# Row decays by small transfers, and a newly laid out order, in a fused linear attention and feed-forward kernel

## The chip, the core and the metric

The kernel runs on one core of a Trainium2 chip, in one launch. The metric is device time in microseconds (us) for one execution; the time before is the median of three. Profiles are of one execution each; their span runs from the first to the last recorded instruction and is a little shorter than the execution's time.

## The reference

Two layers follow each other. The first is a linear attention with a gate for each key element (4 batches, 8 heads, 768 steps, 48 elements a head); the second a gated feed-forward layer (3072 tokens, width 384, hidden width 1536).

```python
f = 1.0 / (1.0 + np.exp(-f_logit))
for t in range(S):
    state = f[:, :, t, :, None] * state + np.einsum('bhd,bhe->bhde', k[:, :, t], v[:, :, t])
    y[:, :, t] = np.einsum('bhd,bhde->bhe', q[:, :, t], state)
x = y.transpose(0, 2, 1, 3).reshape(B * S, H * D)
out = (np.maximum(x @ w_gate, 0.0) * (x @ w_val)) @ w_out
```

All inputs and the output are float32. The kernel multiplies in bf16.

## The kernel before

**Steps, positions, units.** Time is cut into 6 chunks of 128 steps. The work goes in 6 steps c = 0 to 5 of 4 positions b = 0 to 3 each, w = 4c + b. In steps 2 to 5 position b is batch b and the chunk is c. In steps 0 and 1 two positions form a unit: two chunks of one batch, with rows interleaved, so that a load reads 384 bytes a row. Unit 0 is positions 0 and 1 of step 0, unit 1 positions 2 and 3, units 2 and 3 lie in step 1.

**Attention, `front` and `back` (or `unit`).** ScalarE forms log(1 + exp(-f)) (L484, L487). TensorE sums it over the chunk with a triangular matrix (L514; L505 for units) and, with four one-column matmuls (L517; L509 for units), over the whole chunk. ScalarE takes exp(+) for k (L528, `ek`) and exp(-) for q (L530, `eq`), both into the tile `expo`, and from the whole sums the decays of the state (L545; L538 for units) into the tile `dec`. GpSimd (L552) or VectorE (L553) multiplies q and k by them into the tile `hats`. The hats are turned by TensorE (L564) in steps 0 and 1, and by a transposing DMA on SyncE's queue (L572) from step 2 on. Then come the scores (L596; L662 for units), the mask on VectorE (L604, L669), the output y and the state product (L757, L784; L684, L707, L720 for units), and the state update (L454, L458, L460), which reads `dec`.

**Feed-forward.** The four outputs of a step form a group of 512 tokens. For each of 12 hidden blocks there are three gate matmuls and three value matmuls (both L804), a relu on ScalarE (L809) or VectorE (L810) and a product on VectorE (L812). Each output of 128 tokens takes 12 matmuls, in three parts of four (L825), an eviction (L831, L832) and a store (L835). In group 0 the first four hidden blocks are done for each unit by itself, with 256 columns.

**What sets the order.** Each engine runs a list of operations written out by number in `ORDER`. `Plan.link` finds the dependencies from the tiles that an operation reads and writes, `lay_out` places the operations and gives the PSUM banks from `BANKS`, and `waits` makes the semaphore waits. An entry such as `~2512` stands for two matmuls on zeros with 512 columns, which keep TensorE busy. `HELD` adds a dependency by hand: the operation at the left waits for the one at the right. Loads of q, k, v and f go out from SyncE's list or ScalarE's (L408 for units, L413 after), weights from GpSimd's (L435). A list is served in order: what waits at its head holds back all behind it. In the holds before, q of unit 0 (on ScalarE's list) waits for a memset, q of unit 2 for the output of unit 1's second half, v of unit 3 for a transpose of unit 3, and the weight loads `wv2+2`, `wv8+4` and `wo0+4` for operations of group 0.

Weights come in pieces: `wg2+2` is hidden blocks 2 and 3 of the gate, `wg4+4` blocks 4 to 7, and so on.

Of the kernel before, what the change touches and what calls it, by code (L numbers as in the profile page):

```python
# [11 lines left out]
NB, NE, NH, NQ, NM, NV, NA, NN, NS, NX, NG, NR, NO = 3, 3, 6, 6, 5, 6, 3, 4, 2, 2, 2, 4, 3  # L12
UNITS = 4
PE_HATS = set(range(0, 8))
# [11 lines left out]
        45, ~60100, 74, 85, ~3512, 82, ~3512, 90, 80, 92, 121, ~1512, 95, 110, 101, 126, ~4512, 116, ~2512, 100, 128,  # L26
# [14 lines left out]
    ],  # L41
    "ACT": [
# [9 lines left out]
    ],  # L52
    "DVE": [
# [11 lines left out]
    ],  # L65
    "POOL": [
# [4 lines left out]
    ],  # L71
# [9 lines left out]
    48: 10, 57: 114, 60: 140, 67: 284, 69: 164, 70: 185,  # L81
# [161 lines left out]
def bass_hgrn2_outer__then__ffn_reglu_kernel(  # L243
# [11 lines left out]
    C = 128  # L255
# [17 lines left out]
    expo = sb("expo", [128, NE, 2, HD], F32)  # L273
# [14 lines left out]
    decs = sb("dec", [128, NA, B, NP, 2], F32)  # L288
# [6 lines left out]
    tlow = [sb(f"tlow{i}", [128, C], BF16) for i in range(2)]  # L295
    pair = sb("pair", [128, 2], BF16)
    zeros = sb("zeros", [128, 512], BF16)
# [36 lines left out]
    fill("DVE", "zeros", zeros[:], 0.0, 256, -30)  # L334
# [109 lines left out]
    def hq_(i):  # L444
        return f"hq{i}"
# [509 lines left out]
```

## Time and profile before

| | |
|---|---|
| time, median of 3 | 192.87 us (192.62 to 193.22) |
| profiled execution | 193.01 us; span 191.3 us |
| TensorE busy | 180.6 us, 94% of the span |
| VectorE, ScalarE, GpSimd busy | 137.4, 92.0, 59.2 us |
| granted TensorE clock | 1.00 |
| DMA | 32.43 MB moved, 25.95 MB read from HBM |

Engines in the profile: PE is TensorE's matmuls, PEld its weight loads, DVE VectorE, ACT ScalarE, POOL GpSimd, SP SyncE. A row of a group gives the line, the engine, the operation, the tiles and shapes with their count, then busy us and mean ns of one, then the idle time before them and what ended it. A row of the chain or of the timeline gives the start and the length in us. q1 is the queue of SyncE's DMAs, q10 of ScalarE's, q0 of GpSimd's.

### The profile page before, as it was taken

To read this page: it belongs to the slowest core of one execution; us is meant where nothing else is said; L and a number is where in the kernel's file an instruction comes from. 1 tells how busy PE (TensorE), PEld (TensorE's weight loads), DVE (VectorE), ACT (ScalarE), POOL (GpSimd) and SP (SyncE) were. 2 spreads that over 40 slices of the span, in tenths; PEclk is the share of its full clock that TensorE was granted. 3 is DMA by queue.
4 is the path that set the end of the run, shared out by engine and by line. 5 is a ranking of instruction groups with operands and counts; after the bars stand their busy time and mean duration, and the time that the engine had idled before them with its cause. 6 is when DMAs were issued, how large, how long until landed. Compare 5 with 4: busy or idle time off the path is not lost.

```text
span 191.3 us, 4793 instructions
## 1 busy us (share of the span) xinstructions
PE 180.6 (94%) x1977; PEld 108.4 (57%) x1996; DVE 137.4 (72%) x249; ACT 92.0 (48%) x200; POOL 59.2 (31%) x88
## 2 busy tenths in 40 slices
PE   7597999989899999999999999999999999999994
PEld 7364785455655556655555654556656554455562
DVE  4299877986758778669868779988688485655620
ACT  3969663264477546497654574372233132301112
POOL 5638531741036702047371610492600000000000
PEclk9999999999999999999999999999999999999999
DMA  6999999969999999989999999999763300000223
GB/s 163 318 296 216 159 209 264 161 123 251 225 221 206 240 201 246 235 191 200 197 182 215 245 175 175 243 251 178 98 151 108 99 4 0 3 0 0 109 98 126
DMA packets 110278, 32.43 MB, mean 170 GB/s; under 512 B 103472, under 2 KB 110000, under 8 KB 110256
## 3 DMA queue, kind: packets, MB, share of 16 engines
q1 hardware_dynamic: 88960, 25.04, 61.7%
q0 software_dynamic: 3744, 3.54, 12.2%
q10 hardware_dynamic: 17552, 3.54, 10.0%
q8 instruction: 16, 0.26, 0.6%
q14 instruction: 6, 0.05, 0.1%
HBM read 25.95 MB, written 4.72 MB: 160 GB/s over the span
## 4 chain that ended last, share of the span: by engine, by line
PE 85%; DVE 8%; DMA 3%; issue 2%; ACT 0%; DVEq 0%; ACTq 0%
PE ps L804 46%; PE ps L825 25%; DVE hats L553 4%; DMA q_in<-in_q_dram 3%; PE ps L596 2%; PE ps L757 2%; PE ps L564 2%; PE ps L514 1%; DVE gT L812 1%; PE ps L662 1%; PE ps L684 1%; PE ps L784 1%; DVE ptm L669 1%; PE ps L768 1%; PE ps L764 1%
## 5 line engine op out<-in xcount | busy, mean ns | idle before, releaser
L812 DVE TENSOR_TENSOR gT<-relu,ps 128x512 bf16<-128x512 bf16 (+1 forms) x76 | 47.7, 653 | 19.7 <-PE ps L804 17.5
L804 PE MATMUL ps<-xT,wv 128*128 128x512 bf16 (+1 forms) x220 | 53.6, 367 | 0.6 <-issue 0.2
L804 PE MATMUL ps<-xT,wg 128*128 128x512 bf16 (+1 forms) x219 | 52.6, 368 | 0.6
L825 PE MATMUL ps<-wo,gT 128*128 128x384 bf16 (+2 forms) x300 | 52.0, 320 | 0.0
L809 ACT ACTIVATE relu<-ps 128x512 bf16<-128x512 f32 (+1 forms) x42 | 23.9, 576 | 47.8 <-PE ps L804 24.2
L825 PEld LDWEIGHTS ps<-wo,gT 128*128 128x128 bf16 x300 | 27.7, 98 | 18.3
L804 PEld LDWEIGHTS ps<-xT,wg 128*128 128x128 bf16 x228 | 23.6, 108 | 20.5 <-issue 0.4
L804 PEld LDWEIGHTS ps<-xT,wv 128*128 128x128 bf16 x228 | 23.3, 108 | 18.3
L552 POOL TENSOR_TENSOR hats<-q_in,expo 128x384 bf16<-128x384 f32 x17 | 17.9, 1058 | 30.2 <-DMA q_in<-in_q_dram 12.2
L810 DVE TENSOR_SCALAR relu<-ps 128x512 bf16<-128x512 f32 (+1 forms) x34 | 21.7, 654 | 5.4 <-PE ps L804 5.3
L552 POOL TENSOR_TENSOR hats<-k_in,expo 128x384 bf16<-128x384 f32 x17 | 17.7, 1050 | 21.2 <-ACT expo L528 14.9
L604 DVE TENSOR_TENSOR ptm<-ps,tri 128x512 bf16<-128x512 f32 x32 | 20.5, 684 | 5.1 <-PE ps L596 5.1
L831 ACT ACTIVATE osb<-ps 128x384 f32<-128x384 f32 (+1 forms) x16 | 7.6, 484 | 25.0 <-PE ps L825 22.2
L528 ACT ACTIVATE expo<-ps 128x384 f32<-128x384 f32 x24 | 11.7, 496 | 6.1 <-DVE hats L553 2.6
L530 ACT ACTIVATE expo<-ps 128x384 f32<-128x384 f32 x24 | 11.8, 492 | 2.0 <-PE ps L517 1.9
L460 POOL TENSOR_TENSOR st<-ssum,dec 128x384 bf16<-128x384 f32 x10 | 8.6, 864 | 10.0 <-DVE ssum L458 10.0
L669 DVE TENSOR_TENSOR ptm<-ps,tmask 128x512 bf16<-128x512 f32 x16 | 10.0, 678 | 2.1 <-PE ps L662 2.1
L484 ACT ACTIVATE f_in<-f_in 128x768 f32<-128x768 f32 x12 | 10.1, 840 | 2.8 <-DMA f_in<-in_f_logit_dram 2.8
L458 DVE TENSOR_TENSOR ssum<-ps,st 128x384 f32<-128x384 f32 x16 | 8.8, 550 | 2.7 <-PE ps L784 2.5
L553 DVE TENSOR_TENSOR hats<-q_in,expo 128x384 bf16<-128x384 f32 x7 | 8.2, 1167 | 3.4 <-DMA q_in<-in_q_dram 3.4
L487 ACT ACTIVATE bneg<-f_in 128x768 bf16<-128x768 f32 x12 | 10.1, 841 | 1.0 <-ACT osb L831 0.8
L564 PE MATMUL ps<-ident,hats 128*128 128x128 bf16 x64 | 5.5, 220 | 4.0 <-DVE hats L553 3.0
(78 smaller groups left out, 159.2 us busy)
## 6 DMA issues: line engine op xcount, KB each, us to landing
v_in<-in_v_dram SPq DMA_DIRECT2D x12, 384.0 KB, 5.5
out_dram<-osb SPq DMA_DIRECT2D x23, 192.0 KB, 2.3
k_in<-in_k_dram SPq DMA_DIRECT2D x10, 384.0 KB, 7.1
q_in<-in_q_dram SPq DMA_DIRECT2D x9, 384.0 KB, 5.8
f_in<-in_f_logit_dram SPq DMA_DIRECT2D x8, 384.0 KB, 4.8
f_in<-in_f_logit_dram ACTq DMA_DIRECT2D x4, 384.0 KB, 6.6
q_in<-in_q_dram ACTq DMA_DIRECT2D x3, 384.0 KB, 5.6
wv<-in_moe_w_val_dram POOLq DMA_DIRECT2D x2, 384.0 KB, 6.7
```

The costliest lines, as they stand in the source:

```text
L484: add(f"ef{c}{b0}", by("ACT", lambda: sc.activation(raw, raw, AF.Exp, scale=-1.0), act_(n)), keys, keys, key=P)
L528: add(f"ek{c}{b}", by("ACT", lambda: sc.activation(ex[:, 1, :], bc.ap[:, 0:HD], AF.Exp, scale=1.0), act_(HD)), [bc], [f"expk{ei}"], key=P + 1)
L530: add(f"eq{c}{b}", by("ACT", lambda: sc.activation(ex[:, 0, :], bc.ap[:, 0:HD], AF.Exp, scale=-1.0), act_(HD)), [bc], [f"expq{ei}"], key=P ...
L552: return {**by("POOL", lambda: gp.tensor_tensor(o, i_, e_, ALU.mult), pool_(HD)), **by("DVE", lambda: ve.tensor_tensor(o, i_, e_, ALU.mult ...
L553: **by("DVE", lambda: ve.tensor_tensor(o, i_, e_, ALU.mult), dve_(HD))}
L604: add(f"m{c}{b}{j}", by("DVE", lambda b=b, j=j, mi=mi: ve.tensor_tensor(ptm[mi][:, j, :, :], s[b, j].ap[:, :].rearrange("p (n t) -> p n t" ...
L669: add(f"m{c}{b2[i]}{j}", by("DVE", lambda i=i, j=j, mask=mask: ve.tensor_tensor(ptm[mi[i]][:, j, :, :], s[j, i].ap[:, :].rearrange("p (n t ...
L804: z = te.matmul(bank.ap[:, 0:n], wt[:, kt, w_cols(j)], xT[xi][:, kt, n0:n1], start=(kt == 0), stop=(kt == NK - 1))
L809: add(f"r{c}{b0}.{j}", {**by("ACT", lambda: sc.activation(rdst, gate.ap[:, 0:n], AF.Relu), act_(n)), **by("DVE", lambda: ve.tensor_scalar_ ...
L810: **by("DVE", lambda: ve.tensor_scalar_max(rdst, gate.ap[:, 0:n], 0.0), dve_(n))}, [gate], [f"relu{ri}"], key=P)
L812: add(f"p{c}{b0}.{j}", by("DVE", lambda: ve.tensor_tensor(gT[gi][:, j, n0:n1], rdst, val.ap[:, 0:n], ALU.mult), dve_(n)), [val, f"relu{ri} ...
L825: z = te.matmul(o.ap[:, 0:e1 - e0], gT[gi][:, j, b * C:(b + 1) * C], wo[:, j, e0:e1], start=(j == 0), stop=(j == NJ - 1))
```

## The change

**Row decays.** For positions w = 8 to 19 (steps 2 to 4) the four one-column matmuls and the ScalarE exponentials into `dec` are left out. The exp(-) of a pair of positions is written into one interleaved tile, element (d, j, position, p), so that one row holds what the decays need: the last row of the chunk is the whole sum. A new operation `xd`, two DMAs a pair of positions, copies that row from partition 127 to 48 partitions each, eight floats to a partition:

```diff
+ROW_DECAYS = set(range(8, 20))
+NEQ = 2
-            if c < NC - 1:
+            if ch < NC - 1 and not rows:
                 for p in range(NP):
                     x = te.matmul(bc.ap[:, HD + p:HD + p + 1], ... ones[:, :])
...
-        ex = expo[:, ei, :, :]
+        ex = (expq[:, eqi, :, :].rearrange("q x h -> q (x h)").rearrange("q (d j x p) -> q x p j d", d=D, x=2, j=2)[:, b % 2, :, :, :] if rows
+              else expq[:, eqi, b % 2, :].rearrange("q (p j d) -> q p j d", p=NP, j=2),
+              expk[:, ei, :].rearrange("q (p j d) -> q p j d", p=NP, j=2))
...
+        elif rows and b % 2:
+            b0, c0 = place(c, b - 1)
+            def decay_rows(eng):
+                for j in range(2):
+                    at, to = expq[C - 1:C, eqi, 0, 2 * NP * j:2 * NP * j + 1], decs[64 * j:64 * j + D, ai, j, b0, 0:1]
+                    x = eng.dma_start(bass.AP(tensor=to.tensor, offset=to.offset, ap=[list(to.ap[0]), [1, 2 * NP]]),
+                                      bass.AP(tensor=at.tensor, offset=at.offset, ap=[list(at.ap[0]), [4 * NP, D], [1, 2 * NP]]))
+            xd = add(f"xd{c}{b - 1}", {**by("SP", ...), **by("ACT", ...)}, [f"expq{eqi}_0", f"expq{eqi}_1", f"dec{ai}"], [f"dec{ai}_{b0}", f"dec{ai}_{bt}"], key=P + 2)
```

**Tiles.** `expo` (three buffers for both kinds) becomes `expk` with two buffers and `expq` with two pairs. `dec` is stored with the head's half ahead of batch and head pair. `zeros` is 128 columns wide and is read repeatedly for wider fills; `tlow` lies in one buffer of `ssum`. `place` and `load` are written so that more units would be possible; with four the addresses are the same.

**Orders, banks, holds.** `ORDER` and `BANKS` are new in full. The parts that the prediction speaks of:

- SyncE's list begins with f of units 0 and 1, then k, v and q of unit 0, q of unit 1, f of units 3 and 2, k and v of unit 1, k of units 2 and 3, q and v of unit 3, q and v of unit 2, then all f, k, q and v of step 2 on its list and f of step 3: 24 loads ahead of the first store. Before, it began with f of units 0 and 1, k and v of unit 0, k, v and q of unit 1, and q of unit 0 was on ScalarE's list.
- `HELD` keeps `wv8+4` (now behind another relu of group 0) and gains k of steps 4 and 5 in one pair each; the holds of q of units 0 and 2, v of unit 3, `wv2+2` and `wo0+4` are gone.
- ScalarE's list begins exp f, log (unit 0), exp f (unit 1), `ek` of position 1, log (unit 1), decays of unit 0, `ek` and `eq` of position 0. Before, `eq` and `ek` of position 0 came right after exp f of unit 1.
- GpSimd's list after the memsets: hat of q 0, `wg2+2`, hat of q 3, `wv2+2`, hats of q 2, k 2, k 3, a state update, `wg0+2`, v, `wv0+2`, v, hats of k 10 and 11, `wg4+4`. Before: `wg2+2`, hat of k 1, k 3, v, `wv2+2`, hat of q 2, `wg0+2`, `wv0+2`, `wv4+4`, `wg4+4`, `wg8+4` (numbers are step and position).
- TensorE's fills are 12, 2, 2, 2 and 9 matmuls of 512 columns, where before there were 60 of 100 and 3, 3, 1, 4 and 2 of 512. The nine stand between the state product of unit 0 and the transposes of unit 1. The transposes of units 2 and 3 stand among and before the projections of group 0's first four blocks; before they stood behind most of group 0's projections.
- Group 0's relus: 12 on ScalarE and 4 on VectorE, before 8 and 8.
- The six `xd` stand on SyncE's list (20/21, 22/23, 32/33) and on ScalarE's (30/31, 40/41, 42/43). The first stands between the first store and the transposes of step 2.

More of the change, by code (lines that the diff above doesn't have):

```diff
@@ L272, in bass_hgrn2_outer__then__ffn_reglu_kernel @@
     bneg = sb("bneg", [128, NB, 2, H, 64], BF16)
-    expo = sb("expo", [128, NE, 2, HD], F32)
+    expk, expq = sb("expk", [128, NE, HD], F32), sb("expq", [128, NEQ, 2, HD], F32)
     hats = sb("hats", [128, NH, 2, H, 64], BF16)
@@ L287, in bass_hgrn2_outer__then__ffn_reglu_kernel @@
     osb = [sb(f"osb{i}", [128, DM], F32) for i in range(NO)]
-    decs = sb("dec", [128, NA, B, NP, 2], F32)
+    decs = sb("dec", [128, NA, 2, B, NP], F32)
     dec = [decs[:, i, :, :, :] for i in range(NA)]
@@ L294, in bass_hgrn2_outer__then__ffn_reglu_kernel @@
     tmask = [sb(f"tmask{i}", [128, C], BF16) for i in range(2)]
-    tlow = [sb(f"tlow{i}", [128, C], BF16) for i in range(2)]
+    tlow = [ssum[NS - 1][:, C // 2 * i:C // 2 * (i + 1)].bitcast(BF16) for i in range(2)]
     pair = sb("pair", [128, 2], BF16)
-    zeros = sb("zeros", [128, 512], BF16)
+    zeros = sb("zeros", [128, 128], BF16)
     banks = [nc.alloc_psum_tensor(f"ps{i}", [128, 512], F32) for i in range(8)]
@@ L332, in select @@
         add("s" + name, by("POOL", lambda: gp.affine_select(out=ap, in_=ap, **kw), (0.24, 0.29)), [name], [name], key=key)
-    fill("DVE", "zeros", zeros[:], 0.0, 256, -30)
+    fill("DVE", "zeros", zeros[:], 0.0, 64, -30)
     fill("POOL", "tri", tri[:], 1.0, 128, -12 if UNITS else -20)
@@ L450, in new_state @@
         t4 = lambda t: t[:, 0:HD].rearrange("p (n j e) -> p n j e", n=NP, j=2)
-        rate = dec[ai][:, b, :, :].unsqueeze(3).to_broadcast([128, NP, 2, D])
+        rate = dec[ai][:, :, b, :].rearrange("q j p -> q p j").unsqueeze(3).to_broadcast([128, NP, 2, D])
         dk = [f"dec{ai}_{b}", f"dec{ai}"]
@@ L470, in front @@
         w = c * B + b
-        two, cc, bt = w < 2 * UNITS, w // 2 // B * 2, w // 2 % B
+        two, (bt, ch) = w < 2 * UNITS, place(c, b)
+        cc = ch - b % 2
         P = w * 10
         bi, bj = (w // 2) % NB, w % 2
-        ei, hi, qi, ai = w % NE, w % NH, w % NQ, c % NA
+        ei, eqi, hi, qi, ai = w % NE, w // 2 % NEQ, w % NH, w % NQ, ch % NA
         fin, kin, qin, vins = (halves(n, slot_of(n, c, b // 2)) if two else ld[n][:, slot_of(n, c, b // 2), :, :, 0:D] for n in "fkqv")
@@ L495, in front @@
         bn = bneg[:, bi, bj, :, :]
+        rows = w in ROW_DECAYS
         onto = two and bj and w // 2 in ONTO
@@ L523, in front @@
         else:
-            add(f"cum{c}{b}", pe(cum, mm(HD) + (mm(1) * 4 if c < NC - 1 else 0)), ["tri", "ones", f"bneg{bi}", f"bn{bi}_{bj}"], [bc],
+            add(f"cum{c}{b}", pe(cum, mm(HD) + (mm(1) * 4 if ch < NC - 1 and not rows else 0)), ["tri", "ones", f"bneg{bi}", f"bn{bi}_{bj}"], [bc],
                 key=P, opens=[bc])
-        ex = expo[:, ei, :, :]
-        add(f"ek{c}{b}", by("ACT", lambda: sc.activation(ex[:, 1, :], bc.ap[:, 0:HD], AF.Exp, scale=1.0), act_(HD)), [bc],
+        ex = (expq[:, eqi, :, :].rearrange("q x h -> q (x h)").rearrange("q (d j x p) -> q x p j d", d=D, x=2, j=2)[:, b % 2, :, :, :] if rows
+              else expq[:, eqi, b % 2, :].rearrange("q (p j d) -> q p j d", p=NP, j=2),
+              expk[:, ei, :].rearrange("q (p j d) -> q p j d", p=NP, j=2))
+        parts = lambda t: t.rearrange("q (p j d) -> q p j d", p=NP, j=2)
+        past = []
+        if w >= 2 * NEQ and rows != (w - 2 * NEQ in ROW_DECAYS):
+            w0 = w // 2 * 2 - 2 * NEQ
+            names = {f"hq{x // B}{x % B}" for x in (w0, w0 + 1)} | {f"xd{w0 // B}{w0 % B}"}
+            past = [o for o in pl.ops if o.name in names]
+        add(f"ek{c}{b}", by("ACT", lambda: sc.activation(ex[1], parts(bc.ap[:, 0:HD]), AF.Exp, scale=1.0), act_(HD)), [bc],
             [f"expk{ei}"], key=P + 1)
-        add(f"eq{c}{b}", by("ACT", lambda: sc.activation(ex[:, 0, :], bc.ap[:, 0:HD], AF.Exp, scale=-1.0), act_(HD)), [bc],
-            [f"expq{ei}"], key=P + 1)
+        add(f"eq{c}{b}", by("ACT", lambda: sc.activation(ex[0], parts(bc.ap[:, 0:HD]), AF.Exp, scale=-1.0), act_(HD)), [bc],
+            [f"expq{eqi}_{b % 2}"], key=P + 1, after=past)
         if two and bj == 0:
@@ L541, in front @@
             add(f"dc{c}{b}", by("ACT", decay2, (0.24, 0.35)), [bc, f"dec{a0}", f"dec{a0 + 1}"], [f"dec{a0}_{bt}", f"dec{a0 + 1}_{bt}"], key=P + 2)
-        elif c < NC - 1 and not two:
+        elif rows and b % 2:
+            b0, c0 = place(c, b - 1)
+            assert c0 == ch and bt == b0 + 1
+            def decay_rows(eng):
[3 more added lines that the diff above has]
+                                      bass.AP(tensor=at.tensor, offset=at.offset, ap=[list(at.ap[0]), [4 * NP, D], [1, 2 * NP]]))
+                    if j == 0:
+                        x.then_inc(xd.sem, 16)
+                return x
+            xd = add(f"xd{c}{b - 1}", {**by("SP", lambda: decay_rows(sy), (0.8, 0.8)), **by("ACT", lambda: decay_rows(sc), (0.8, 0.8))},
+                     [f"expq{eqi}_0", f"expq{eqi}_1", f"dec{ai}"], [f"dec{ai}_{b0}", f"dec{ai}_{bt}"], key=P + 2)
+            dma(xd, f"dec{ai}_{b0}", "SP", 6, 0.013)
+            slots[f"dec{ai}_{b0}"][1] += 16
+            xd.goal += 16
+        elif rows:
+            pass
+        elif ch < NC - 1 and not two:
             def decay():
                 for j in range(2):
-                    x = sc.activation(dec[ai][64 * j:64 * j + 64, b, :, j], bc.ap[64 * j:64 * j + 64, HD:HD + NP], AF.Exp, scale=-1.0)
+                    x = sc.activation(dec[ai][64 * j:64 * j + 64, j, bt, :], bc.ap[64 * j:64 * j + 64, HD:HD + NP], AF.Exp, scale=-1.0)
                 return x
-            add(f"dc{c}{b}", by("ACT", decay, (0.23, 0.34)), [bc, f"dec{ai}"], [f"dec{ai}_{b}"], key=P + 2)
+            add(f"dc{c}{b}", by("ACT", decay, (0.23, 0.34)), [bc, f"dec{ai}"], [f"dec{ai}_{bt}"], key=P + 2)
         def scaled(src, xh, xe):
-            o, e_ = hats[:, hi, xh, :, 0:D], ex[:, xe, :].rearrange("p (h d) -> p h d", h=H)
-            i_ = src[:, b % 2, :, :]
+            o, e_ = hats[:, hi, xh, :, 0:D].rearrange("q (p j) d -> q p j d", p=NP), ex[xe]
+            i_ = src[:, b % 2, :, :].rearrange("q (p j) d -> q p j d", p=NP)
             return {**by("POOL", lambda: gp.tensor_tensor(o, i_, e_, ALU.mult), pool_(HD)),
@@ L554, in front @@
         add(f"hk{c}{b}", scaled(kin, 1, 1), in_k("k") + [f"expk{ei}", f"hats{hi}"], [hk_(hi)], key=P + 2)
-        add(f"hq{c}{b}", scaled(qin, 0, 0), in_k("q") + [f"expq{ei}", f"hats{hi}"], [hq_(hi)], key=P + 2)
+        add(f"hq{c}{b}", scaled(qin, 0, 0), in_k("q") + [f"expq{eqi}_{b % 2}", f"hats{hi}"], [hq_(hi)], key=P + 2)
         if w in PE_HATS:
@@ L736, in back @@
         P = w * 10
+        bt, ch = place(c, b)
         hi, qi, mi, vi, xi = w % NH, w % NQ, w % NM, w % NV, c % NX
@@ L768, in natural @@
                 z = te.matmul(y.ap[:, h * D:(h + 1) * D], ptm[mi][:, h % 2, h // 2, :], vp[:, at:at + D],
-                              start=(c == 0 and h == 0), stop=True, skip_group_check=True)
+                              start=(ch == 0 and h == 0), stop=True, skip_group_check=True)
             return z
@@ L887, in run @@
                     eng.wait_ge(sems[d.eng], d.val)
+                n = fill % 1000
+                row = zeros[:, 0:n] if n <= 128 else zeros[:].unsqueeze(1).to_broadcast([128, n // 128, 128])
                 for _ in range(fill // 1000):
-                    te.matmul((op.opens[0].ap if op.opens else banks[7])[:, 0:fill % 1000], zeros[:, 0:128], zeros[:, 0:fill % 1000],
+                    te.matmul((op.opens[0].ap if op.opens else banks[7])[:, 0:n], zeros[:], row,
                               start=True, stop=True, skip_group_check=True)
```

38 lines of the change are left out of this document (22 added, 16 removed), and 102 rows, old and new, of tables (BANKS, ORDER).

## The prediction

> **What bounds the kernel now.** I read the page's shares first, then the busy time by stretches, TensorE's waits, the chain of the first 10 us, and last the DMA queues.
>
> ```profile
> span 191.3 us, 4793 instructions
> PE 180.6 (94%) x1977; PEld 108.4 (57%) x1996; DVE 137.4 (72%) x249; ACT 92.0 (48%) x200; POOL 59.2 (31%) x88
> PE 85%; DVE 8%; DMA 3%; issue 2%; ACT 0%; DVEq 0%; ACTq 0%
> ```
>
> The profiled execution took 193.01 us, 1.7 more than its span and 0.14 more than the median of 192.87; sums below are against 193.0. TensorE sets the time. Its idle time lies where the stretches show it (columns: length, then busy us of PE, PEld, DVE, ACT, POOL, then granted clock, DMA share, GB/s):
>
> ```profile
> 5.00:10.00 5.00, 2.72 (x35) 1.64 (x33) 1.79 (x3) 4.47 (x9) 2.81 (x7) 1.00 1.17 312
> 15.00:20.00 5.00, 3.54 (x140) 2.54 (x141) 4.97 (x9) 4.67 (x9) 4.76 (x6) 1.00 0.99 182
> 30.00:40.00 10.00, 9.78 (x55) 5.10 (x54) 9.96 (x13) 4.03 (x9) 5.71 (x7) 1.00 1.02 196
> 40.00:50.00 10.00, 9.22 (x120) 5.69 (x120) 7.58 (x16) 4.51 (x9) 2.01 (x4) 1.00 0.93 197
> 50.00:60.00 10.00, 9.40 (x228) 5.80 (x229) 6.78 (x13) 6.83 (x14) 3.30 (x4) 1.00 1.36 231
> 60.00:70.00 10.00, 9.95 (x55) 5.33 (x55) 7.43 (x13) 5.54 (x15) 5.38 (x6) 1.00 0.98 199
> ```
>
> Three regions lose time: the front of the first two units (to 20 us), 30 to 60 us (1.6 us idle: 0.22, 0.78, 0.60), and the drain. From 60 us on almost nothing is idle. So a change can gain only by taking matmuls away, or by ending waits before 60 us:
>
> ```profile
> PE ps L564 <- DVE hats L553: 3.0, 2, 1.9
> PE ps L564 <- DVE gT L812: 0.8, 1, 0.8
> PE ps L684 <- issue: 0.5, 1, 0.5
> ```
>
> L564 are the transposes of the scaled q and k: TensorE waits for VectorE's multiplications. VectorE is the crowded engine there (9.96 of 10 us in 30 to 40).
>
> **Part 1: row decays, steps 2 to 4.** The change takes out L517, four one-column matmuls behind each of 12 cumulative sums, and L545, the ScalarE exponentials that read them.
>
> ```profile
> 53.28 0.34 PE L514 MATMUL ps<-bneg,tri 128*128 128x384 bf16 x1
> 53.45 0.24 PE L517 MATMUL ps<-ones,bneg 128*128 128x1 bf16 x4
> 53.55 0.81 PE L825 MATMUL ps<-wo,gT 128*128 128x384 bf16 x4
> L517 PE MATMUL ps<-ones,bneg 128*128 128x1 bf16 x48 | 2.9, 164 | 0.0
> L545 ACT ACTIVATE dec<-ps 64x4 f32<-64x4 f32 x24 | 4.0, 166 | 1.1 <-PE ps L517 0.9
> ```
>
> Matmuls overlap, so 2.9 us busy is the upper bound. The four start at 53.45 and the next operation at 53.55: 0.10 us a sum, 12 x 0.10 = 1.2 us of TensorE, nearly all of it after 53 us where TensorE is full. I take -1.2 (bounds -2.9 and 0). ScalarE loses 4.0 us of work, worth nothing by itself at 48% busy.
>
> It adds six transfers of two DMAs each (three pairs on SyncE's queue, three on ScalarE's). They read one row of the exponentials; what waits for them is the state update, a whole set of masks and scores later. Behind the first of them on SyncE's queue stand the transposes of step 2, whose hats are ready later than those exponentials anyway. The trace has no DMA that small. The nearest is the smallest store, which lands in 1.6 us; the transposes, which lie behind them on SyncE's queue, take 3.3:
>
> ```profile
> out_dram<-osb SPq DMA_DIRECT2D x1, 64.0 KB, 1.6
> qkT<-hats SPq DMA_TRANSPOSE x16, 3.3
> L552 POOL TENSOR_TENSOR hats<-q_in,expo 128x384 bf16<-128x384 f32 x17 | 17.9, 1058 | 30.2 <-DMA q_in<-in_q_dram 12.2 <-ACT f_in L484 11.3 <-ACT expo L530 6.7
> 175.59 1.30 PE ps L825 x8
> 149.72 9.66 PE ps L804 x44
> ```
>
> The tightest place I find in the new order is the pair 42/43: between its cumulative sums and its scores lie 16 projections of three L804 matmuls and 4 output parts of four L825 matmuls, 48 x 0.22 + 16 x 0.16 = 13.1 us. The chain in it is four exponentials (2 us), two decay issues, GpSimd's hats (1.06 each, one behind a value load), the transposes (two issues, 3.3 to land): 9 to 10 us. Cover of 3 us, so zero; if it is gone, its overrun is paid in full. The two buffers of k's exponentials instead of three make an exponential wait for the hat two positions before it, which stands ahead of it by several GpSimd operations: zero by the same cover.
>
> The row layout makes q's exponentials a stride of 64 bytes for ScalarE's write and for the multiplication. No row shows that stride; bounds are 0 and a doubling of 1.06 us, and I take the middle, +0.5 a hat, hidden by those 3 us. [...]
>
> **Part 2: unit 0's loads in one queue, and ScalarE's new order.**
>
> ```profile
> 2.54 5.55 DMA q_in<-in_q_dram
> 8.19 1.29 DVE hats L553
> 9.52 0.40 PE ps L564 x4
> 7.10 0.87 ACT L528 ACTIVATE expo<-ps 128x384 f32<-128x384 f32 x2
> 5.10 0.84 ACT L487 ACTIVATE bneg<-f_in 128x768 bf16<-128x768 f32 x1
> 14.80 0.36 ACT L538 ACTIVATE dec<-ps 64x8 f32<-64x8 f32 x2
> q1 hardware_dynamic: 1357, 0.52, 101.7%
> q1 hardware_dynamic: 861, 0.32, 117.1%
> 11.86 0.64 PE L662 MATMUL ps<-qkT 48*64 48x128 bf16 x32
> 19.84 0.50 PE L804 MATMUL ps<-xT,wg 128*128 128x256 bf16 x3
> ```
>
> Today q of unit 0 lands last (8.1) and starts the chain. As fifth load in SyncE's queue it is complete after 5 x 0.39 MB. The queue moved 0.52 MB by 4 us (first q1 row, 2 to 4 us) and 0.32 MB a us when full (second, 8 to 9 us): 4 + 1.45 / 0.32 = 8.5. But ScalarE, free of its first exponential at 7.1, now runs the second logarithm and the decays before the exponentials of position 0: 7.1 + 0.8 + 0.3 + 0.9 = 9.1, so the later load is covered. GpSimd then multiplies until 10.1, and with the transposes and copies the first scores (L662) come at 11.7 to 12.3, against 11.86. The second half's k comes ninth instead of fifth (about 14.5), and GpSimd's hats behind it push the first projection (L804) to about 20.3, against 19.84. The nine idle fills of 512 columns ahead of those transposes (9 x 0.22 = 2.0 us from about 13.2) end before the hats, so cost nothing unless the state product ahead of them is late. By then the new order has also done three cumulative sums, 1.2 us of work. Net -0.7; chains added by hand leave small waits out, so I take -0.3, bounds -1.0 and +0.8.
>
> **Part 3: 28 to 55 us, and the weights.** VectorE is relieved: of group 0's 16 relus it keeps 4 instead of 8 (ScalarE takes 12), and of the first four units' 16 hats 5 instead of 8. The transposes of units 2 and 3 stand some 10 us of TensorE work earlier. So the L564 waits there (1.1 for hats, 0.8 for gT) should shrink: of the 1.6 us idle I take 0.9 away (bounds 0 and 1.6). Against that stands the loss of two holds. SyncE now keeps back q of unit 2, with all that is queued behind it, to 23.98 us, and v of unit 3 to 42.3; the new order issues 24 loads without a wait, beside the weights.
>
> ```profile
> 23.98 0.37 SPq L408 DMA_DIRECT2D q_in<-in_q_dram  x1
> 42.30 0.99 SPq L408 DMA_DIRECT2D v_in<-in_v_dram  x2
> q0 software_dynamic: 580, 0.57, 120.1%
> ...
> q1 hardware_dynamic: 1393, 0.53, 99.6%
> 28.83 0.81 PE L804 MATMUL ps<-xT,wg 128*128 128x512 bf16 x3
> q0 software_dynamic: 3744, 3.54, 12.2%
> wg<-in_moe_w_gate_dram POOLq DMA_DIRECT2D x2, 384.0 KB, 9.0
> ```
>
> The third and fourth rows are queues in 24 to 27 and in 28 to 30 us (packets, MB, share of the engines): a load issued at 23.98 got nothing while the weights (q0) were queued, and all engines after. Requests are served in blocks, roughly as issued, so a weight waits for the two or three loads ahead of it and then has the engines. With GpSimd's work before it the first 384 KB weight goes out at about 21.9 (19.4 today) and lands, by the same 9.0 or, without the other weights ahead of it, some 2 less, at 28.9 to 30.9; its first use is due at about 28.6 (28.83 today). GpSimd's hat of q, position 11, waits for the fifteenth load, about 31, which may cost TensorE 0.6. Together +0.8 (0 to +3). Part 3 is -0.9 + 0.8 = -0.1.
>
> Sum: -1.2 - 0.3 - 0.1 = -1.6; 193.0 - 1.6 = 191.4. The drain keeps its last three steps, zero.
>
> **Rivals.** (a) *Weights late, slower.* If the unheld loads get their share first, the last gate and value columns land 3 to 6 us after their use is due (about 36 to 41 us), TensorE waits there, and nothing returns it: 191.4 and 3 to 6 gives 194.4 to 197.4, 195 the nearest. It decides once each weight lands over 8 us after its issue. For: 24 loads of 0.39 MB and the weights (3.54 MB written, twice that read as float32) need about 50 us at 0.32 MB a us. Against: the blocks above. [...] Chance 0.20. (b) *The saving is eaten*: new waits of 1 to 2 us in the re-laid order, as the old one has 1.6; 192.3 to 193.8, chance 0.14. (c) *The stride slows the hats* until the scores of pair 42/43 wait: 3 us of cover gone and 2.4 more, 193.8; for it only the doubled hat, four of them in a row; against it GpSimd's 31% share. Chance 0.04. (d) *All early waits end*: a further 1.5, 189.9; chance 0.12.
>
> **How the numbers follow.** The forecast, 190.4 to 192.3, has 0.50. About 0.3% (0.6 us) can be told from no change. Faster: 0.50 + 0.12 = 0.62. Of (b) 0.10 lies within 0.3%, 0.04 above; slower is 0.20 + 0.04 + 0.04 = 0.28. The range 189.9 to 195.2 leaves out part of (d) and the worse part of (a), under 2 in 10.
>
> **What would show it.** Right: L517 gone and TensorE's busy time 1 us less after 53 us; first projection near 20.3; 30 to 60 us with under 1.5 us idle. Wrong: L804 of group 0 waiting for wg or wv between 28 and 45 us; transposes waiting for the small DMAs on SyncE's queue; L596 (scores) idle in step 4; hats above 1.5 us.

## The result, and the profile after

The changed kernel takes 190.8 us (median of 4, 190.59 to 191.51) against 192.93 before (192.62 to 193.22), a ratio of 0.989 [0.9852, 0.9927]. On another chip, with more runs of the kernel before beside it, it took 191.27 (six runs) and the ratio was 0.9885 [0.9847, 0.9923]. The forecast was 191.4 in 189.9 to 195.2. (The first run of `e8_relu_dve` took 314.01 us at a granted clock of 0.56; the ratios in this document leave it out, and with it a few executions that were slower at a slightly lower clock, which the medians include.)

The page after, its span and shares, for an execution of 190.59 us:

```profile
span 188.9 us, 4607 instructions
PE 182.4 (97%) x1902; PEld 104.9 (56%) x1902; DVE 133.9 (71%) x246; ACT 91.9 (49%) x179; POOL 60.7 (32%) x88
```

TensorE's busy time is higher than before, though 48 matmuls are gone. That is no riddle: fills take 9.0 us where they took 7.5, and the trace of before holds 439 of the 456 gate and value projections, that of after all. So busy totals of the two aren't compared; idle stretches and experiments are. (A record that is missing leaves a gap of only 0.05 us, as at 35.85 us of the kernel before, where two of three projections are recorded.) The same view by stretches as in the prediction, from 20 us on:

```profile
20.00:25.00 5.00, 3.66 (x99) 2.51 (x99) 4.06 (x8) 3.30 (x8) 5.00 (x8) 1.00 1.30 267
30.00:40.00 10.00, 10.00 (x114) 5.67 (x113) 8.78 (x17) 4.07 (x9) 3.09 (x5) 1.00 1.22 211
40.00:50.00 10.00, 10.00 (x225) 6.01 (x224) 6.62 (x13) 6.84 (x12) 0.00 (x0) 1.00 0.97 191
50.00:60.00 10.00, 10.00 (x52) 5.01 (x51) 5.75 (x9) 5.65 (x11) 8.03 (x9) 1.00 1.12 218
```

The 1.6 us of idle TensorE between 30 and 60 us are gone (0.1 of them were missing records), and from there to 180 us nothing is idle. One hole is new, 20 to 25 us. TensorE's waits name it:

```profile
PE ps L842 <- DMA wg<-in_moe_w_gate_dram: 1.1, 1, 1.1
PE ps L601 <- POOL hats L589: 0.2, 1, 0.2
```

L842 is the line of the projections (L804 before), L601 that of the transposes (L564). The transposes' 3.8 us of waiting for VectorE has become 0.2 for GpSimd, and a wait for a gate weight is new. But 3.0 of the 3.8 stood in the front, at 9.52 us (1.85) and, in the kernel before, here:

```profile
17.64 0.61 PE L564 MATMUL ps<-ident,hats 128*128 128x128 bf16 x8 [1.17 <-DVE hats L553]
```

Only the 0.8 for `gT`, at 40.78 us, lie between 30 and 60 us. In the front other work and fills stand where those 3.0 us were. The changed kernel, in order of time:

```profile
11.76 0.64 PE L699 MATMUL ps<-qkT 48*64 48x128 bf16 x32 [0.60 <-DVE qkT L605]
19.93 0.83 PE L842 MATMUL ps<-xT,wg 128*128 128x256 bf16 x6
23.30 0.83 PE L842 MATMUL ps<-xT,wg 128*128 128x256 bf16 x6 [1.13 <-DMA wg<-in_moe_w_gate_dram]
```

The first scores come at 11.76 and the first projection at 19.93 us, as before to 0.1 us, with three more cumulative sums done. The wait at 23.30 is for `wg0+2`, issued at 16.77 and landed at 23.3, 6.5 us later.

### The profile page after: what moved, and what is told of

Same layout as the page of the kernel before. It is cut to its first block, busy times and chain, and to the rows that moved or that the text cites. A ratio compares the mean times of both kernels' runs of the same rounds, so it can differ in the third digit from the quotient of the medians.

```text
span 188.9 us, 4607 instructions
## 1 busy us (share of the span) xinstructions
PE 182.4 (97%) x1902; PEld 104.9 (56%) x1902; DVE 133.9 (71%) x246; ACT 91.9 (49%) x179; POOL 60.7 (32%) x88
## 4 chain that ended last, share of the span: by engine, by line
PE 86%; DMA 6%; SPq 3%; POOL 2%; ACT 1%; issue 0%
PE ps L842 49%; PE ps L863 25%; DMA wg<-in_moe_w_gate_dram 3%; SPq L411 3%; DMA f_in<-in_f_logit_dram 3%; PE ps L633 2%; PE ps L795 2%; POOL hats L589 2%; PE ps L524 1%; PE ps L822 1%; PE ps L721 1%; PE ps L601 1%; PE ps L806 1%; PE ps L802 1%; PE ps L699 1%; PE ps L757 0%
## 5 line engine op out<-in xcount | busy, mean ns | idle before, releaser
L842 PE MATMUL ps<-xT,wv 128*128 128x512 bf16 (+1 forms) x228 | 56.1, 368 | 0.0
L842 PE MATMUL ps<-xT,wg 128*128 128x512 bf16 (+1 forms) x228 | 54.7, 368 | 1.2 <-DMA wg<-in_moe_w_gate_dram 1.1
L847 ACT ACTIVATE relu<-ps 128x512 bf16<-128x512 f32 (+1 forms) x47 | 26.7, 577 | 49.0 <-PE ps L842 46.7
L842 PEld LDWEIGHTS ps<-xT,wg 128*128 128x128 bf16 x228 | 23.7, 108 | 21.3 <-DMA wg<-in_moe_w_gate_dram 1.5
L842 PEld LDWEIGHTS ps<-xT,wv 128*128 128x128 bf16 x228 | 23.5, 108 | 18.9
L848 DVE TENSOR_SCALAR relu<-ps 128x512 bf16<-128x512 f32 (+1 forms) x29 | 18.9, 658 | 9.7 <-PE ps L842 9.6
L589 POOL TENSOR_TENSOR hats<-k_in,expk 128x384 bf16<-128x384 f32 x17 | 16.9, 999 | 26.2 <-ACT expk L546 26.1
L589 POOL TENSOR_TENSOR hats<-q_in,expq 128x384 bf16<-128x384 f32 x15 | 17.8, 1190 | 19.0 <-ACT expq L548 12.5
L641 DVE TENSOR_TENSOR ptm<-ps,tri 128x512 bf16<-128x512 f32 x32 | 20.3, 683 | 2.3 <-PE ps L633 2.1
L869 ACT ACTIVATE osb<-ps 128x384 f32<-128x384 f32 (+2 forms) x18 | 8.6, 480 | 22.1 <-PE ps L863 20.7
L548 ACT ACTIVATE expq<-ps 128x384 f32<-128x384 f32 x24 | 15.5, 669 | 0.0
L546 ACT ACTIVATE expk<-ps 128x384 f32<-128x384 f32 x24 | 11.8, 498 | 2.0 <-PE ps L524 1.3
L646 ACT ACTIVATE xT<-ps 128x384 bf16<-128x384 f32 x10 | 5.1, 535 | 9.6 <-PE ps L795 5.9
L619 POOL CAST vpad<-v_in 128x384 bf16<-128x384 f32 x12 | 6.9, 588 | 8.9 <-DMA v_in<-in_v_dram 8.9
## 6 DMA issues: line engine op xcount, KB each, us to landing
out_dram<-osb SPq DMA_DIRECT2D x23, 192.0 KB, 2.2
```

What stands on the lines that cost most here:

```text
L546: add(f"ek{c}{b}", by("ACT", lambda: sc.activation(ex[1], parts(bc.ap[:, 0:HD]), AF.Exp, scale=1.0), act_(HD)), [bc], [f"expk{ei}"], key=P ...
L548: add(f"eq{c}{b}", by("ACT", lambda: sc.activation(ex[0], parts(bc.ap[:, 0:HD]), AF.Exp, scale=-1.0), act_(HD)), [bc], [f"expq{eqi}_{b % 2 ...
L589: return {**by("POOL", lambda: gp.tensor_tensor(o, i_, e_, ALU.mult), pool_(HD)), **by("DVE", lambda: ve.tensor_tensor(o, i_, e_, ALU.mult ...
L641: add(f"m{c}{b}{j}", by("DVE", lambda b=b, j=j, mi=mi: ve.tensor_tensor(ptm[mi][:, j, :, :], s[b, j].ap[:, :].rearrange("p (n t) -> p n t" ...
L842: z = te.matmul(bank.ap[:, 0:n], wt[:, kt, w_cols(j)], xT[xi][:, kt, n0:n1], start=(kt == 0), stop=(kt == NK - 1))
L847: add(f"r{c}{b0}.{j}", {**by("ACT", lambda: sc.activation(rdst, gate.ap[:, 0:n], AF.Relu), act_(n)), **by("DVE", lambda: ve.tensor_scalar_ ...
```

## The experiments

| kernel | median us | before, same chip | ratio of the two |
|---|---|---|---|
| e1_keep_sums | 192.38 | 193.16 | 0.9975 [0.9944, 1.0005] |
| e2_no_rows | 192.22 | 193.16 | 0.9964 [0.9937, 0.999] |
| e3_rows_old | 204.12 | 193.16 | 1.0566 [1.0503, 1.0628] |
| e6_wg_first | 191.08 | 193.16 | 0.9911 [0.9879, 0.9943] |
| e3b_rows_old_act | 197.86 | 193.42 | 1.0192 [1.0143, 1.0242] |
| e5_old_no_holds | 196.50 | 193.42 | 1.0136 [1.0092, 1.0179] |
| e8_relu_dve | 193.88 | 193.42 | 1.0024 [1.0001, 1.0046] |
| e9_weights_first | 190.58 | 193.42 | 0.9851 [0.9814, 0.9887] |
| a0_changed | 191.27 | 193.78 | 0.9885 [0.9847, 0.9923] |
| e10_hold_step2 | 190.77 | 193.78 | 0.9857 [0.9823, 0.9892] |
| e8b_relu_dve | 193.15 | 193.78 | 0.9987 [0.995, 1.0023] |
| e7_q0_act | 191.75 | 193.78 | 0.9908 [0.9873, 0.9944] |

**The matmuls, put back into the changed kernel.**

```diff
-            if ch < NC - 1 and not rows:
+            if ch < NC - 1:
```

> The changed kernel (190.8 us), with the 48 one-column matmuls of steps 2 to 4 put back; their results are not read. Theory (TensorE is never idle from 30 us on, so its work sets the time): 12 x 0.10 us more, 192.0. Rival (the one-column matmuls were hidden and the gain comes from the new order alone): 190.8.

It took 192.38, by the ratios 0.85% or 1.6 us more than the changed kernel, so the one-column matmuls cost what the theory said and a little over. The start times in its timeline confirm the 0.10 us a sum (L524 is the sum, L527 the four matmuls):

```profile
49.99 0.24 PE L527 MATMUL ps<-ones,bneg 128*128 128x1 bf16 x4
50.09 0.32 PE L524 MATMUL ps<-bneg,tri 128*128 128x384 bf16 x1
...
59.12 0.84 PE L842 MATMUL ps<-xT,wv 128*128 128x512 bf16 x3 [0.83 <-DVE relu L848]
```

The last row is what the matmuls cost beside their own time: a projection at 59 us now waits 0.8 us for a relu.

**The new order without row decays.**

```diff
-ROW_DECAYS = set(range(8, 20))
+ROW_DECAYS = set()
```

with the 24 exponentials into `dec` back in ScalarE's list, behind those of k and q, and no `xd`.

> The new order without row decays: sums by matmuls, decays by ScalarE right behind the exponentials of their position, no small transfers, no interleaved layout. Theory: only the matmuls count, 192.0, as in e1. Rival 1 (ScalarE's 4 us of decays matter too): 192.5 or more. Rival 2 (the interleaved layout slows ScalarE and the hats and costs time): 191.5 or less.

192.22, near the theory's 192.0 and between the two rivals. It is 1.4 us more than the changed kernel, and 0.7 less than before (0.2 to 1.2 by its interval). Here the split is clean: no new wait of any size, and TensorE's row has the difference (182.4 in the changed kernel):

```profile
PE 184.0 (97%) x1950; PEld 106.3 (56%) x1950; DVE 133.7 (70%) x246; ACT 92.3 (48%) x203; POOL 58.1 (31%) x88
```

So, taken away from the changed kernel, the row decays are two thirds of the gain, and the order without them is one third. Between the two kernels only the row layout and the decays differ, which prices the layout too. First the groups of this kernel, then those of the changed one:

```profile
L548 ACT ACTIVATE expq<-ps 128x384 f32<-128x384 f32 x24 | 11.6, 497 | 0.1
L589 POOL TENSOR_TENSOR hats<-q_in,expq 128x384 bf16<-128x384 f32 x15 | 15.5, 1038 | 17.9 <-ACT expq L548 12.6 <-DMA q_in<-in_q_dram 5.2
```

```profile
L548 ACT ACTIVATE expq<-ps 128x384 f32<-128x384 f32 x24 | 15.5, 669 | 0.0
L589 POOL TENSOR_TENSOR hats<-q_in,expq 128x384 bf16<-128x384 f32 x15 | 17.8, 1190 | 19.0 <-ACT expq L548 12.5 <-DMA q_in<-in_q_dram 6.3
```

The strided write costs ScalarE 3.9 us over 12 exponentials (0.8 us each instead of 0.5), and the 4.0 us of decay exponentials that it saves are gone with it: ScalarE's total is 91.9 against 92.3. Of the seven strided hats of q on GpSimd four take 1.19 us, two 1.5 and one 1.8, instead of 1.0.

**The row decays in the old order, with the transfers on SyncE's list.** Order, banks and holds of before; k's exponentials have three buffers, q's two pairs as in the changed kernel; each transfer stands just ahead of the first transpose of its pair (lists by names):

```diff
 # SyncE
+xd20 ahead of the first of xh20, xh21; xd22, xd30, xd32, xd40, xd42 likewise
 # ScalarE
-dc20 dc21 ... dc43
```

> The old order with row decays alone (three buffers of k's exponentials; each small transfer on SyncE's list ahead of the first transpose of its pair). Theory: 192.9 - 1.2 = 191.7. Rival (in an order not made for them the transfers or the slower layout delay the transposes of steps 2 to 4, and scores wait): 192.9 or more.

204.12, 11 us slower than before. The theory fell. The rival's time came, but not by late transposes or scores: ScalarE's waits and one row of its timeline tell why:

```profile
ACT expq L539 <- DMA dec<-expq: 10.1, 2, 6.6
...
94.84 0.81 ACT L539 ACTIVATE expq<-ps 128x384 f32<-128x384 f32 x1 [6.58 <-DMA dec<-expq]
...
PE ps L833 <- ACT osb L860: 4.5, 1, 4.5
PE ps L833 <- ACT expq L539: 2.5, 1, 2.5
```

A pair's tile comes free only when its transfer has landed, and that transfer stood behind loads and stores in SyncE's list. So an exponential waits 6.6 us, and behind it in ScalarE's list wait an eviction and relus, for which TensorE waits. That is 7.0 us of waiting. After the longer wait the granted clock fell as well:

```profile
95.00:102.00 7.00, 5.97 (x18) 2.45 (x19) 0.56 (x1) 3.15 (x7) 0.00 (x0) 0.51 0.98 218
```

Seven us at 0.51 are about 3.4 us of full clock lost. So, by this estimate, about a third of the 9.5 us by which this execution is longer (202.53 against 193.01) comes through the clock.

**The same, with the transfers on ScalarE's list**, right behind the exponentials that they read. The buffers are those of the run above (the three buffers that the expectation gives to q's exponentials are k's).

```diff
 # SyncE
-xd20 xd22 xd30 xd32 xd40 xd42
 # ScalarE
+each behind the second exponential of q of its pair
```

> The order, banks and holds of the kernel before, with the row decays of steps 2 to 4; all six small transfers stand on ScalarE's list, right behind the exponentials that they read, and q's exponentials have three buffers. Theory (what made the earlier attempt slow was the place of the transfers on SyncE's list, behind loads and transposes, and not the transfers or the layout): nothing is queued ahead of a transfer, so it lands 3 to 5 us after its exponentials, TensorE loses 1.2 us of one-column matmuls, and the time is 191.3 to 192.2 us, with ScalarE's exponentials waiting for a transfer by under 1 us. Rival 1 (the layout or the transfers themselves cost time in an order not made for them): 192.9 or more, up to the 204 of the earlier attempt, with TensorE waiting for q's exponentials or for GpSimd's hats of q. Rival 2 (the old order's idle time swallows the saving): 192.9 within 0.5, TensorE 1 us less busy and 1 us more idle.

197.86: the theory fell. Rival 1's time came, but by another wait than it names (TensorE for q's exponentials or hats): the transfers land soon (2.7 us median), but their issue occupies ScalarE. First ScalarE here, then the same place in the kernel before:

```profile
57.75 2.24 ACTq L557 DMA_DIRECT2D dec<-expq  x2
60.03 0.84 ACT L486 ACTIVATE bneg<-f_in 128x768 bf16<-128x768 f32 x1 [2.32 <-issue]
...
61.02 0.32 PE L514 MATMUL ps<-bneg,tri 128*128 128x384 bf16 x1 [1.99 <-ACT bneg L486]
```

```profile
57.30 0.84 ACT L487 ACTIVATE bneg<-f_in 128x768 bf16<-128x768 f32 x1
```

The two small DMAs hold the list for 2.24 us, the logarithm comes 2.7 us later than before, and the cumulative sum waits 2 us for it. That is one of several such places; TensorE is also idle by 1.1 us in 90 to 100 us and 0.9 in 100 to 110, and not each of these is traced. What is shown: the row decays are worth 1.4 us in the order laid out for them, and cost 4 to 11 us in one that isn't.

**The old order without its holds on loads.** Rival (a), priced where it can be.

```diff
-    48: 10, 57: 114, 60: 140, 67: 284, 69: 164, 70: 185,
+    48: 10, 57: 114, 69: 164, 70: 185,
```

(60 is q of unit 2, 67 v of unit 3.)

> The kernel before, without its holds of q of unit 2 and v of unit 3, so that SyncE issues these loads and all behind them without a wait, beside the weights. Theory (a weight in GpSimd's queue is served before the loads that are queued beside it, so the loads suffer and the weights do not): 192.5 to 194, TensorE's waits for wg or wv together under 1 us, and loads of q and f that take 10 us and more to land. Rival (the queues share, so unheld loads delay the weights; rival a of the prediction): 195 to 198, with L804 waiting 2 us or more for wg or wv between 18 and 45 us.

196.5, by the ratio 2.6 us slower than before: the rival holds. TensorE waits for weights, and the last three of the four gate loads (issued 17.0 to 20.1 us) take longer to land. The first block is this run, the second the kernel before:

```profile
PE ps L804 <- DMA wg<-in_moe_w_gate_dram: 1.7, 1, 1.7
PE ps L804 <- DMA wv<-in_moe_w_val_dram: 0.9, 1, 0.9
...
DMA to landing us min/median/max: 8.0/12.6/14.5
```

```profile
DMA to landing us min/median/max: 5.4/8.2/9.9
```

The queues in 20 to 25 us show how (packets, MB, share of the engines), here and then in the kernel before:

```profile
q0 software_dynamic: 909, 0.48, 68.8%
q1 hardware_dynamic: 1664, 0.63, 56.2%
```

```profile
q0 software_dynamic: 1207, 0.88, 122.5%
```

With the loads held back the weights have the engines to themselves, 0.88 MB in 5 us; with loads queued beside them they get about half of that, 0.48 MB. Here the queues share, 68.8% to 56.2%.

**Two weight loads earlier in the changed kernel.** First `wg0+2` alone:

```diff
 # GpSimd
-hk03 sd10 wg0+2 v02
+hk03 wg0+2 sd10 v02
```

> The changed kernel with one entry moved on GpSimd's list: the weight load of gate blocks 0 and 1 ahead of a state update of 0.84 us. Theory (the 1.1 us that TensorE waits for that weight at 22 us is set by when it is issued): it lands 0.8 us earlier, 190.0 to 190.1. Rival (it is set by what is queued ahead in the DMA engines, or the state update becomes late): 190.8 or more.

191.08 and 0.9911 [0.9879, 0.9943], no better than the changed kernel, so the forecast time was missed. The weight did land 0.9 us earlier, as the theory said, but the gain went into the next one: the wait at 22 us falls from 1.13 to 0.30, and the next weight, `wg4+4`, is waited for by 0.57 at 29.3, where it still lands at 29.2. Then both:

```diff
-wv0+2 v03 hk10 mones hk11 wg4+4
+wv0+2 v03 hk10 mones wg4+4 hk11
```

> The changed kernel with two weight loads one place earlier on GpSimd's list: wg0+2 ahead of a state update, and wg4+4 ahead of a hat of k. The run with only the first of them moved showed the wait for wg0+2 down from 1.13 to 0.3 us, and a new one of 0.57 us for wg4+4. Theory (each weight lands about as long after its issue as before, so each comes 1 us earlier): both waits end, 189.9 to 190.4. Rival (the engines are full there, so a weight issued earlier takes the longer, or the hat that is moved back makes the transposes behind it late): 190.8 or more, with TensorE waiting for wv, the next loads or L605's copies instead.

190.58 at 0.9851 [0.9814, 0.9887], the lowest of all. The waits for weights don't end; what was one wait is now three small ones, for the same 1.0 us together:

```profile
PE ps L842 <- DMA wg<-in_moe_w_gate_dram: 0.6, 2, 0.3
PE ps L842 <- DMA wv<-in_moe_w_val_dram: 0.4, 1, 0.4
```

**The changed kernel again, and the step's loads held.** To both moves is added a hold of f of step 2:

```diff
-    69: 185, 649: 800, 797: 615,
+    69: 185, 649: 800, 797: 615, 368: 172,
```

> The changed kernel itself, on the chip of the next three, so that differences of half a us between them can be read: 190.8 us within 0.5.

> The changed kernel with the two weight loads one place earlier, as in the run with both moved (190.6), and f of step 2, the first load behind the units' own, held on SyncE's list until the gate matmuls of group 0's block 3 (about 27.5 us), so that the step's loads stay out of the engines while weights are queued. Theory (loads and weights share the engines, 66% and 63% of them in 20 to 25 us; fewer loads beside them, and the weights land sooner): wg4+4 and wv4+4 land 0.5 to 1.5 us sooner, the waits for wg and wv (1.0 us in that run) end, and f lands no later than before, since its 17 us to land were spent waiting for the engines: 189.6 to 190.3. Rival (the held loads are missed later: f, v and k of step 2 come late, ScalarE's exponentials wait past 45 us): 190.8 or more, with TensorE waiting between 45 and 70 us.

191.27 and 190.77, the second above its forecast. The waits for weights fall to 0.3 for wg and 0.2 for wv, and nothing waits between 45 and 70 us, as the theory said. But the time doesn't fall with them: a new wait stands 100 us later, for a transposing DMA of `xn` on SyncE's queue.

```profile
132.12 0.82 PE L842 MATMUL ps<-xT,wg 128*128 128x512 bf16 x3 [0.77 <-DMA xT<-xn]
```

Whether the hold makes this wait isn't shown: `e7_q0_act` below, which has no such hold, has one of 0.73 us at 133.81. Both versions with earlier weights lie half a us below the changed kernel, less than the intervals can tell apart. That they beat the kernel before is shown, that they beat the changed one isn't.

**Four relus of group 0 back on VectorE.**

```diff
 # ScalarE
-r00.4 r00.7 r00.9 r00.11
 # VectorE
+r00.4 r00.7 (behind r00.5), r00.9 (behind the product of block 5), r00.11 (of block 6)
```

> The changed kernel with four relus of group 0 (unit pair 0, blocks 4, 7, 9 and 11) put back from ScalarE to VectorE, which then has eight as before. Theory (VectorE's relief ended the waits between 30 and 60 us): VectorE gets 4 x 0.65 = 2.6 us more in 30 to 60 us, TensorE waits 0.5 to 1.5 us there again, 191.3 to 192.3. Rival (the earlier transposes ended them, and VectorE has slack): 190.8 within 0.3 and no idle TensorE from 30 to 60 us.

> The changed kernel with the four relus of group 0 on VectorE once more, for its profile at full clock. It took 3 us, twice what was expected. Theory: VectorE's 2.6 us more delay the products and copies in 30 to 60 us one for one, with TensorE waiting there 2.5 to 3.5 us for gT, relu or qkT. Rival: the cost lies later (the order from 60 us on is laid out for other times), with TensorE idle past 60 us. 193.9 within 0.6.

193.88 on one chip, 193.15 on the other, where the changed kernel took 191.27: +1.9 us (by the ratios 1.0%). The first expectation was too small, the second (193.9 within 0.6, 2.5 to 3.5 us of waiting) too large; both had the place right. TensorE's wait and the stretches:

```profile
PE ps L843 <- DVE ptm L707: 1.4, 1, 1.4
...
30.00:40.00 10.00, 8.62 (x105) 4.67 (x104) 8.17 (x16) 2.22 (x5) 3.24 (x6) 1.00 1.22 210
40.00:50.00 10.00, 9.65 (x152) 5.33 (x152) 8.51 (x15) 4.60 (x7) 0.00 (x0) 1.00 0.96 187
```

It is the mask behind the scores (`ptm`) that comes late, not a gate product or a relu as the second expectation had it: it stands in VectorE's list behind the relus. From 50 to 180 us nothing is idle. So without VectorE's relief this stretch waits again, 1.7 us in all (1.38 and 0.35). It is another wait than those of the kernel before, and what the earlier transposes add was not tried by itself. Nor need 1.9 us be what moving them brought: the list into which they are put back was laid out without them, and the whole new order without row decays brings 0.7.

**q of unit 0 back on ScalarE's queue.**

```diff
 # ScalarE
+Lq0.0 first
 # SyncE
-Lf0.0 Lf0.2 Lk0.0 Lv0.0 Lq0.0
+Lf0.0 Lf0.2 Lk0.0 Lv0.0
```

> The changed kernel with q of unit 0 at the head of ScalarE's list, as before, instead of fifth on SyncE's. Theory (ScalarE's exponential that feeds the first hat ends at 9.1, so where q comes from is covered): q lands at 8 to 9 us, the first scores stay at 11.8 within 0.2, 190.8 within 0.3. Rival 1 (q lands some 1 us later or earlier and moves the chain of the front): the first scores and the time move by the same amount, 190.3 or 191.5. Rival 2 (with q off SyncE's queue every load behind it is issued 1.2 us sooner, and the weights wait longer): wg0+2 lands later, TensorE waits over 1.5 us for it, 191.2 to 191.8.

191.75, 0.5 more than the changed kernel on this chip, within the intervals. But the front moves by more than that, and by a way that none of the three theories had: not q is late, but f. ScalarE's first exponential and the first scores, then the same exponential in the changed kernel:

```profile
5.35 0.84 ACT L493 ACTIVATE f_in<-f_in 128x768 f32<-128x768 f32 x1 [3.27 <-DMA f_in<-in_f_logit_dram]
...
12.95 0.64 PE L699 MATMUL ps<-qkT 48*64 48x128 bf16 x32 [0.60 <-DVE qkT L605]
...
26.50 0.62 PE L601 MATMUL ps<-ident,hats 128*128 128x128 bf16 x8 [1.48 <-DVE hats L590]
```

```profile
4.33 0.84 ACT L493 ACTIVATE f_in<-f_in 128x768 f32<-128x768 f32 x1 [2.25 <-DMA f_in<-in_f_logit_dram]
```

With q issued at 0.83 us, beside the first loads of f, f lands 1.0 us later; the first scores come 1.2 us later. That q takes a share of the engines from f there is the author's reading of these times. The wait for `wg0+2` shrinks by 0.9 in return, since the projections come later and the weight doesn't. In the kernel before, q was issued at 2.54, held by a memset; there ScalarE's logarithm of f began at 5.10 (6.29 here, 5.27 in the changed kernel), so that hold and the place in SyncE's queue do the same for f.

## Why the forecast held, step by step

**What bounds it.** Right: the gain lies in matmuls taken away and in waits before 60 us; from 60 to 180 us the kernel before had next to nothing idle.

**Part 1, -1.2.** Right in kind, somewhat small: 1.4 and 1.6 by the two kernels that put the matmuls back. Worked out from the starts of two neighbouring operations (0.10 us a sum) it was nearer than the 2.9 us of the group's busy time. In `e1_keep_sums` a wait of 0.8 us is part of the excess; the 0.2 in `e2_no_rows`, which has no such wait, is within the intervals. That TensorE's busy time falls by 1 us, one of the signs of being right, shows there: 184.0 against 182.4.

**The small transfers and the layout, 0.** Right in this order, as no scores wait in step 4 and TensorE is never idle from 30 to 180 us. The sizes, in the changed kernel:

```profile
dec<-expq SPq DMA_DIRECT2D x6, 1.5 KB, 4.6
dec<-expq ACTq DMA_DIRECT2D x6, 1.5 KB, 3.5
```

They land in 1.8 to 7.3 us, at the upper end far more than the 1.6 and 3.3 of the rows that stood for them. The stride was priced at +0.5 us a hat. It measured 0.2 in four of the seven strided hats on GpSimd (1.19 us against 1.0 without the stride), 0.5 in two (1.49 and 1.50) and 0.8 in one (1.81). That last one is a sign of being wrong that the prediction named, a hat above 1.5 us; it came and cost TensorE nothing. The step that was missing is that a transfer holds something: ScalarE's list while it is issued (2.24 us for two, at 57.75 us in `e3b_rows_old_act`), and the pair of exponentials until it has landed (an exponential waited 6.58 us for that before 94.84 us in `e3_rows_old`). "Zero by the same cover" was true of the order, which leaves room for it, not of the operation: without that room 4 and 11 us.

**Part 2, -0.3.** First scores 11.76 (11.7 to 12.3 forecast), first projection 19.93 (20.3). q of unit 0 was covered as said: it landed 4.8 us after its issue at 4.33, about 9.1, when its exponential ended, so with nothing to spare. What the step did not see is that q's place matters for f, above. What part 2 brought by itself was not tried; an estimate is 0.2 us, the 0.7 of the order without row decays less the 0.5 of part 3 (1.6 - 1.1).

**Part 3, -0.9 + 0.8.** Its sum was too small by 0.4 us, and one of its rows was misread: the 1.1 for hats that it counts among the waits of 28 to 55 us stood at 17.64 us, in the front. In 30 to 60 us TensorE waited for `gT` (0.81), in the middle of an output for a cause that the profile doesn't name (0.55 before 52.05 us, the third row of the prediction's waits) and in smaller gaps. These waits went wholly, 1.6 and not 0.9, and the relus moved to ScalarE are needed for it (1.7 of waiting when four were put back). The loss to weights was 1.1 where 0.8 was taken, but it was another weight: `wg0+2` with 192 KB at 23.3 us, not the first of 384 KB, which landed at about 29.3, just as its first use began at 29.39. The hat of position 11 cost TensorE nothing.

The reason that was given against rival (a), that requests are served in blocks and a weight then has the engines, holds in some stretches and not in others. Over 20 to 25 us of the changed kernel the shares of the queues are about even:

```profile
q1 hardware_dynamic: 2375, 0.90, 65.9%
q0 software_dynamic: 828, 0.42, 62.8%
```

But us by us they take turns, and a weight then does have the engines. Here are 21 to 22 us and 23 to 24 us:

```profile
q0 software_dynamic: 370, 0.18, 135.0%
q1 hardware_dynamic: 23, 0.01, 4.0%
...
q1 hardware_dynamic: 790, 0.30, 108.5%
q0 software_dynamic: 28, 0.01, 10.4%
```

In `e5_old_no_holds`, with a burst of weights queued, the two move the same number of packets from 25 to 30 us, and the weights, with about 0.96 KB a packet against 0.38, move 0.74 MB to the loads' 0.29:

```profile
q0 software_dynamic: 773, 0.74, 87.2%
q1 hardware_dynamic: 771, 0.29, 33.0%
```

From 20 to 25 us of that run the counts are not equal (909 and 1664), and in the 24 to 27 us of the kernel before, a load that was already issued, at 23.98, moved nothing (of the two queues only q0 moved packets, 580). So the runs show even shares in some stretches and turns in others; what decides between the two isn't shown.

What kept the weights in time is seen in their issue: the old order issues five in a row, 17.0 to 20.9 us, uses the first of them from 22.5 us on, and needs the engines whole for that (with loads beside them TensorE waited 2.6 us, in `e5_old_no_holds`); the new one issues its first two at 10.2 and 12.2 and the next at 16.8, 18.0, 21.8, 25.0 and 26.8, and a share of the engines serves them all but for `wg0+2`. That this spacing is the cause is argued from these issue times and from `e5_old_no_holds`, not tried by itself. The loads pay too: the two of f of step 2, issued from 24.12, took 17.2 us to land in the median, and nothing on TensorE waited for them.

**The sum.** -1.6 forecast, -2.1 by the medians and -2.4 between the two profiled executions: part 1 short by 0.2 to 0.4, part 3 by 0.4. That the total came this near is in part luck: both terms of part 3 were too small, and they have opposite signs. The parts don't add up exactly when they are tried one by one (0.7 for the order alone, 1.9 for four relus in it). `e6_wg_first` shows one way in which this happens: a wait that was shortened uncovered the next.

**The rivals.** (a) is a real mechanism, 2.6 us in the old order (with the fall of the clock that is told below), and is paid here with the 1.1 us of one weight. (b) and (c) didn't come. (d), that all early waits end, came true from 30 us on and not before.

## What to carry to other kernels

An operation that is free in an order laid out for it can cost several times its saving in another (here 4 to 11 us for a saving of 1.4), so look, for each DMA that is added to a compute engine's list or to a queue with loads, at what is queued behind its issue and what its source tile keeps from being reused. Weights and loads in different queues shared the engines in the old order: in 5 us the weights moved 0.88 MB alone, and 0.48 and 0.74 MB beside loads in `e5_old_no_holds`. So issue each weight early and apart (argued here, not tried by itself), or hold the loads back where the weights go out in a burst. Where an engine is full for 10 us, look at what a few evictions moved to an idler one would bring: here the four that were moved back cost 1.9 us, the one-column matmuls 1.4 to 1.6.

## What the runs showed of the hardware that was not expected

The issue of two DMAs of 1.5 KB each held ScalarE's list for 2.24 us (57.75 us in `e3b_rows_old_act`), as long as the issue of a 384 KB load held SyncE's at 15.02 us in the changed kernel (2.18 us; the two issued from 4.33 us took 1.15 each).

ScalarE's write of 384 float32 a partition at a stride of 64 bytes took 0.82 to 0.89 us, that of a row without a gap about 0.49. VectorE's multiplication with the strided operand took 0.80 us at 85.77 us, and 0.55 at the same place of `e2_no_rows` (87.09), where there is no stride.

In two runs TensorE's granted clock fell after a wait. In `e5_old_no_holds` TensorE was busy for 0.8 us of 3 before 25 us, and then:

```profile
25.00:26.00 1.00, 0.86 (x29) 0.53 (x36) 0.00 (x0) 0.00 (x0) 0.00 (x0) 0.68 1.22 205
26.00:27.00 1.00, 1.00 (x70) 0.73 (x52) 0.17 (x1) 0.00 (x0) 0.00 (x0) 0.50 1.20 205
27.00:28.00 1.00, 1.00 (x12) 0.58 (x5) 0.86 (x2) 0.60 (x1) 0.00 (x0) 0.50 1.21 209
28.00:29.00 1.00, 1.00 (x7) 0.73 (x6) 0.00 (x0) 0.69 (x3) 0.00 (x0) 0.62 1.20 206
```

At 0.68, 0.50, 0.50 and 0.62 of full clock these four us lose 1.7, on top of the 2.6 of waiting. Together that is more than the 3.5 us by which this execution is longer (196.55 against 193.01); where the rest came back was not traced. In `e3_rows_old` a wait of 4.5 us was followed by 0.51 over seven us. In `e7_q0_act` a wait of 1.48 us at 25 us was followed by no such fall (1.00 in each us from 25 to 31). How long a wait has to be for it isn't shown, and the stretch before the fall in `e5_old_no_holds` was not wholly idle.
